# Gated linear attention and a bilinear feed-forward layer on one core: the first two chunks stage by stage over the batch rows, weights issued between their loads, and the y matmuls of a row grouped by tile mode

## The chip, the cores and the metric

The kernel runs on one core of one Trainium2 chip. The metric is the device time of one execution in microseconds (us); the median of several executions is given with the range. A verdict compares the mean time of one kernel's fast runs with the mean of the fast runs of the kernel before in the same rounds; so a ratio is not quite the ratio of the medians that are quoted. A run is called slow when it lies over 1.5% above the fastest of the same kernel, and slow runs take no part in a ratio. The granted clock is the share of full speed at which TensorE was let run; "half clock" below is a granted clock of 0.5.

## The reference, cut to what matters

```python
# q, k, v, alpha: (4, 8, 768, 48) float32, alpha in 0.8 .. 1.0
for t in range(S):
    state = alpha[:, :, t, :, None] * state + einsum('bhd,bhe->bhde', k[:, :, t], v[:, :, t])
    y[:, :, t] = einsum('bhd,bhde->bhe', q[:, :, t], state)
x = y.transpose(0, 2, 1, 3).reshape(3072, 384)
out = ((x @ w_a) * (x @ w_b)) @ w_out      # w_a, w_b: 384 x 1536, w_out: 1536 x 384
```

## The kernel before

The 768 tokens are cut into six chunks of 128. Within a chunk the recurrence becomes matmuls: with beta the running product of alpha (the exponential of a cumulative sum of logarithms), Q' = q·beta and K' = k/beta, y is the masked product of scores with v plus Q' times the state that came in. Heads are padded from 48 to 64 columns so that two fit on 128 partitions; there are four such pairs. A "row" below is one of the four batch rows of a chunk. A "bank" is one of the named tiles ("t1", "t2", "se", "so", four of "f") that TensorE writes results into and that another engine must have read before they are written again. A matmul's tile mode is the part of TensorE's array that it uses: the full width, or 48 of its columns.

```python
def stA(ch, b):                                     # cumulative sum of the logs, two exponentials
    p = ps.tile([C, 512], F32, name="t2")[:, :H * D]
    nc.tensor.matmul(p, lhsT=ut_f32, rhs=ch.la[:, b], start=True, stop=True)
    nc.scalar.activation(out=ch.beta[:, b], in_=p, func=AF.Exp)
    nc.scalar.activation(out=ch.invb[:, b], in_=p, func=AF.Exp, scale=-1.0)
def stB(ch, b):                                     # K' and Q' on GpSimd, v to bf16 on VectorE
    ...
def stC(ch, b):                                     # 8 transposes into bank "t1", one copy (qk)
    ...
def stD(ch, b):                                     # 8 score matmuls into "se" and "so", two masks
    ...
    nc.vector.tensor_mul(ch.me, se, mask4)
    nc.vector.tensor_mul(ch.mo, so, mask4)
def stY(ch, b):
    y = ps.tile([C, P2, C], F32, name="t2")
    for p in range(P2):                             # a full-width matmul and two 48-wide ones, in turn
        nc.tensor.matmul(y[:, p, :], lhsT=Sb[:, b, p, :], rhs=ch.qkD[:, 0, p, :], start=True, stop=False, ...)
        nc.tensor.matmul(y[0:D, p, :], lhsT=ch.vb[:, b, 2 * p, :], rhs=ch.me[:, p, :], start=False, stop=True, ...)
        nc.tensor.matmul(y[DP:DP + D, p, :], lhsT=ch.vb[:, b, 2 * p + 1, :], rhs=ch.mo[:, p, :], ...)
    nc.scalar.activation(out=ch.xT[:, :, b, :], in_=y[:, :KT, :], func=AF.Copy)
    nc.scalar.activation(out=ch.y3[:, b, :], in_=y[:, KT, :], func=AF.Copy)
def fill(ch):                                       # the 4th head pair goes into the padding rows of xT
    for r in range(2):
        for t in range(KT):
            nc.sync.dma_start(out=ch.xT[r * DP + D:(r + 1) * DP, t], in_=ch.y3[...])
...
for b in range(B):                                  # chunk 0, one row after the other
    logs(c0, b); stA(c0, b); stB(c0, b)
    ...
    if b == 1: load_ab(0)                           # a quarter of w_a and w_b, by columns
    if b == 2: load_ab(1)
    stC(c0, b); stD(c0, b); stY(c0, b)
fill(c0)
for b in range(B): stK(c0, b)                       # state update
load_ab(2); load_ab(3)
for i in range(4): load_o(i)
logs(chunks[1]); ...
for c in range(NCH):                                # dense layer of chunk c, attention of c+1 between its blocks
    for f in range(NFF):
        ff_a(ch, f); ...; ff_b(ch, f)
    for m in range(B):
        ff_o(ch, m)
        if n2 is not None and m >= 2: stA(n2, m - 2); stB(n2, m - 2)
```

("..." marks what is left out.) The dense layer of a chunk is twelve blocks (three matmuls with w_a, three with w_b) and four output groups of twelve matmuls with w_out.

Of the kernel before, what the change touches and what calls it, by code (L numbers as in the profile page):

```python
# [15 lines left out]
def kernel(  # L16
# [43 lines left out]
    Qp, Kp = [], []  # L60
    for i in range(2):
        t = cst.tile([C, B, H, DP], BF16, name=f"Qp{i}")
        nc.vector.memset(t, 0.0)
        Qp.append(t)
        t = cst.tile([C, B, H, DP], BF16, name=f"Kp{i}")
        nc.vector.memset(t, 0.0)
        Kp.append(t)

    wa_t = cst.tile([128, KT, d_ff], BF16, name="wa_t")
    wb_t = cst.tile([128, KT, d_ff], BF16, name="wb_t")  # L70
    wo_t = cst.tile([128, NFF, d_model], BF16, name="wo_t")
    WS = d_ff // 4

    def load_ab(i):
        fs = slice(i * WS, (i + 1) * WS)
        for w, t in ((moe_w_a, wa_t), (moe_w_b, wb_t)):
            two = w[:KT * 2 * D, fs].rearrange("(t r d) f -> r d t f", r=2, d=D)
            rest = w[KT * 2 * D:, fs].rearrange("(r t g) f -> r g t f", r=2, g=G)
            for r in range(2):
                nc.gpsimd.dma_start(out=t[r * DP:r * DP + D, :, fs], in_=two[r])  # L80
                nc.gpsimd.dma_start(out=t[r * DP + D:(r + 1) * DP, :, fs], in_=rest[r])

    def load_o(i):
        n = NFF // 4
        nc.gpsimd.dma_start(out=wo_t[:, i * n:(i + 1) * n, :],  # L85
                            in_=moe_w_out[i * n * 128:(i + 1) * n * 128, :].rearrange("(k p) f -> p k f", p=128))


    class Chunk:
# [8 lines left out]
    def alloc_loads(ch):  # L98
        ch.a = ld.tile([C, B, H, D], F32, name="a_t")
        ch.k = ld.tile([C, B, H, D], F32, name="k_t")  # L100
        ch.q = ld.tile([C, B, H, D], F32, name="q_t")
        ch.v = ld.tile([C, B, H, D], F32, name="v_t")

    def load(ch, b):
        if b == 0:
            alloc_loads(ch)
        sl = slice(ch.c * C, (ch.c + 1) * C)
        for t, src in ((ch.a, alpha), (ch.k, k), (ch.q, q), (ch.v, v)):
            nc.sync.dma_start(out=t[:, b], in_=src[b, :, sl, :].rearrange("h s d -> s h d"))

    def logs(ch, b=None):
        if b is None or b == 0:
            ch.la = wk.tile([C, B, H * D], F32, name="la")
            ch.beta = wk.tile([C, B, H * D], F32, name="beta")
            ch.invb = wk.tile([C, B, H * D], F32, name="invb")
            ch.vb = wk.tile([C, B, H, D], BF16, name="vb")
            ch.bl = wk.tile([C, B, P2], F32, name="bl")
            ch.xT = wk.tile([128, KT, B, C], BF16, name="xT")
            ch.y3 = wk.tile([128, B, C], BF16, name="y3")
        if b is None:  # L120
            nc.scalar.activation(out=ch.la.rearrange("p b f -> p (b f)"), in_=ch.a.rearrange("p b h d -> p (b h d)"), func=AF.Ln)
        else:
            nc.scalar.activation(out=ch.la[:, b], in_=ch.a[:, b].rearrange("p h d -> p (h d)"), func=AF.Ln)  # L123

    def stA(ch, b):
        p = ps.tile([C, 512], F32, name="t2")[:, :H * D]
        nc.tensor.matmul(p, lhsT=ut_f32, rhs=ch.la[:, b], start=True, stop=True)  # L127
        nc.scalar.activation(out=ch.beta[:, b], in_=p, func=AF.Exp)  # L128
        nc.scalar.activation(out=ch.invb[:, b], in_=p, func=AF.Exp, scale=-1.0)  # L129

    def stB(ch, b):
        i = ch.c % 2
        nc.gpsimd.tensor_mul(Kp[i][:, b, :, :D], ch.k[:, b], ch.invb[:, b].rearrange("p (h d) -> p h d", h=H))  # L133
        nc.gpsimd.tensor_mul(Qp[i][:, b, :, :D], ch.q[:, b], ch.beta[:, b].rearrange("p (h d) -> p h d", h=H))  # L134
        nc.vector.tensor_copy(ch.vb[:, b], ch.v[:, b])

    def decay(ch):
# [6 lines left out]
            nc.sync.dma_start(out=ch.bl[r * DP:r * DP + D].rearrange("d b a -> d (b a)"),  # L144
                              in_=row[:, :, r, :].rearrange("o a d -> d (o a)"), allow_slow_non_contiguous=True)

    def stC(ch, b):
        i = ch.c % 2
        t = ps.tile([C, 2, P2, C], BF16, name="t1")
        for p in range(P2):  # L150
            for j, src in enumerate((Qp[i], Kp[i])):
                nc.tensor.transpose(t[:, j, p, :], src[:, b, 2 * p:2 * p + 2, :].rearrange("s h d -> s (h d)"), ident)  # L152
        ch.qk = wk.tile([C, 2, P2, C], BF16, name="qk", bufs=3)
        nc.vector.tensor_copy(ch.qk.rearrange("p j a s -> p (j a s)"), t.rearrange("p j a s -> p (j a s)"))  # L154

    def stD(ch, b):
        se = ps.tile([C, P2, C], F32, name="se")
        so = ps.tile([C, P2, C], F32, name="so")
        for p in range(P2):
            nc.tensor.matmul(se[:, p, :], lhsT=ch.qk[0:DP, 1, p, :], rhs=ch.qk[0:DP, 0, p, :], start=True, stop=True)  # L160
            nc.tensor.matmul(so[:, p, :], lhsT=ch.qk[DP:2 * DP, 1, p, :], rhs=ch.qk[DP:2 * DP, 0, p, :], start=True, stop=True)  # L161
        ch.me = wk.tile([C, P2, C], BF16, name="me")
        ch.mo = wk.tile([C, P2, C], BF16, name="mo")
        nc.vector.tensor_mul(ch.me, se, mask4)  # L164
        nc.vector.tensor_mul(ch.mo, so, mask4)  # L165
        ch.qkD = ch.qk

    def stY(ch, b):
        y = ps.tile([C, P2, C], F32, name="t2")
        for p in range(P2):  # L170
            nc.tensor.matmul(y[:, p, :], lhsT=Sb[:, b, p, :], rhs=ch.qkD[:, 0, p, :], start=True, stop=False, skip_group_check=True)  # L171
            nc.tensor.matmul(y[0:D, p, :], lhsT=ch.vb[:, b, 2 * p, :], rhs=ch.me[:, p, :], start=False, stop=True, skip_group_check=True)  # L172
            nc.tensor.matmul(y[DP:DP + D, p, :], lhsT=ch.vb[:, b, 2 * p + 1, :], rhs=ch.mo[:, p, :], start=False, stop=True, skip_group_check=True)  # L173

        nc.scalar.activation(out=ch.xT[:, :, b, :], in_=y[:, :KT, :], func=AF.Copy)  # L175
        nc.scalar.activation(out=ch.y3[:, b, :], in_=y[:, KT, :], func=AF.Copy)

    def fill(ch):
        for r in range(2):
# [36 lines left out]
    def ff_o(ch, m):  # L216
        op = ps.tile([128, NT], F32, name="f", bufs=4)[:, :d_model]
        for f in range(NFF):
            nc.tensor.matmul(op, lhsT=ch.prod[:, f, m * C:(m + 1) * C], rhs=wo_t[:, f, :], start=(f == 0), stop=(f == NFF - 1))  # L219
        ot = wk.tile([128, d_model], F32, name="ot", bufs=3)  # L220
        nc.scalar.activation(out=ot, in_=op, func=AF.Copy)  # L221
        nc.sync.dma_start(out=out[m * S + ch.c * C:m * S + (ch.c + 1) * C, :], in_=ot)


    for b in range(B):
        load(chunks[0], b)
    for b in range(B):
        load(chunks[1], b)
    c0 = chunks[0]
    for b in range(B):  # L230
        logs(c0, b)
        stA(c0, b)
        stB(c0, b)
        if b == B - 1:
            decay(c0)
        if b == 1:
            load_ab(0)
        if b == 2:
            load_ab(1)
        stC(c0, b)  # L240
        stD(c0, b)
        stY(c0, b)
    fill(c0)
    for b in range(B):
        stK(c0, b)
    load_ab(2)
    load_ab(3)
    for i in range(4):
        load_o(i)
    logs(chunks[1])  # L250
    stA(chunks[1], 0)
    stB(chunks[1], 0)
    stA(chunks[1], 1)
    stB(chunks[1], 1)

    for c in range(NCH):
        ch = chunks[c]
        nx = chunks[c + 1] if c + 1 < NCH else None
        n2 = chunks[c + 2] if c + 2 < NCH else None
        todo = {}  # L260
        if nx is not None:
            todo = {
                0: lambda: stA(nx, 2), 1: lambda: stB(nx, 2), 2: lambda: (stC(nx, 0), stA(nx, 3)),
                3: lambda: (stD(nx, 0), stB(nx, 3), decay(nx)), 4: lambda: stC(nx, 1), 5: lambda: (stY(nx, 0), stK(nx, 0), stD(nx, 1)),
                6: lambda: stC(nx, 2), 7: lambda: (stY(nx, 1), stK(nx, 1), stD(nx, 2)), 8: lambda: stC(nx, 3),
                9: lambda: (stY(nx, 2), stK(nx, 2), stD(nx, 3)), 11: lambda: (stY(nx, 3), fill(nx), stK(nx, 3)),
            }
        for f in range(NFF):
            ff_a(ch, f)
            if n2 is not None and f == 0:  # L270
                for b in range(B):
                    load(n2, b)
            if n2 is not None and f == NFF - 1:
                logs(n2)
            if f in todo:
                todo[f]()
            ff_b(ch, f)
        for m in range(B):
            ff_o(ch, m)
            if n2 is not None and m >= 2:  # L280
                stA(n2, m - 2)
                stB(n2, m - 2)


# [28 lines left out]
```

## Time and profile before

| | before |
|---|---|
| median of 3 (range) | 281.64 us (280.61 to 281.82) |
| span of the profiled execution | 280.6 us |
| TensorE busy | 231.5 us, 82% |
| chunk 0's dense layer begins | 60.83 us |
| chunk 1's dense layer begins | 109.56 us |
| period from one dense layer to the next, chunks 1 to 3 | 36.69 us |
| chunk 4's period; chunk 5 to the end | 33.79; 27.19 us |

Read it as two parts. From 109.56 us to the last store, TensorE is busy for 98% or more of each period, and a period has a price in TensorE work. Before that TensorE waits, and the question is for whom.

### The profile page before, as it was taken

What the parts mean: (1) busy time and instruction counts of PE and PEld (TensorE: products, weight loads), DVE (VectorE), ACT (ScalarE), POOL (GpSimd) and SP (SyncE); (2) the same over time, 40 slices, a digit from 0 to 9 for tenths busy, and PEclk for the clock granted to TensorE, in tenths of its full rate; (3) what the DMA queues carried; (4) which work ended last, traced back from release to release, by engine and by line L of the source; (5) the groups of instructions that cost most, each with busy time, mean ns of one, the idle gap of its engine ahead of it and who ended that gap; (6) DMA issues with size and microseconds to landing.
All of it is one profiled execution on the core that took longest, in us unless ns stands there. A gap on an engine that the chain in (4) does not pass through costs nothing.

```text
span 280.6 us, 4180 instructions
## 1 busy us (share of the span) xinstructions
PE 231.5 (82%) x1520; PEld 120.6 (43%) x1520; DVE 120.3 (43%) x213; ACT 122.8 (44%) x219; POOL 89.7 (32%) x134
## 2 busy tenths in 40 slices
PE   2435344584399999999999999999999999999994
PEld 0203122231245554555544555545555455454452
DVE  7303030422057820867505767047861267503420
ACT  5061533552033367533765336563365644424431
POOL 2217352297942114604127023082040730000000
PEclk9999999999579999999999999999999999999999
DMA  8999961079994005982039940289501200021002
GB/s 155 215 211 208 192 87 2 7 145 209 196 184 66 1 12 158 218 176 19 5 123 205 188 62 2 99 184 204 94 2 52 75 2 0 4 71 56 0 32 84
DMA packets 117503, 28.07 MB, mean 100 GB/s; under 512 B 109221, under 2 KB 117477, under 8 KB 117482
## 3 DMA queue, kind: packets, MB, share of 16 engines
q1 hardware_dynamic: 112298, 24.25, 42.2%
q0 software_dynamic: 5184, 3.54, 8.7%
q8 instruction: 12, 0.20, 0.3%
q14 instruction: 9, 0.07, 0.1%
HBM read 25.98 MB, written 4.75 MB: 110 GB/s over the span
## 4 chain that ended last, share of the span: by engine, by line
PE 76%; POOL 6%; issue 6%; ACT 4%; DMA 3%; DVE 3%; POOLq 0%; DVEq 0%; ACTq 0%
PE f L213 17%; PE f L219 17%; PE f L205 15%; PE t L127 7%; PE t L172 6%; PE t L171 5%; PE t L152 5%; PE se L160 3%; PE t L189 2%; DMA wa_t<-in_moe_w_a_dram 2%; POOL Kp L133 2%; ACT invb L129 2%; POOL Qp L134 2%; DMA a_t<-in_alpha_dram 1%; POOL wo_t L85 1%
## 5 line engine op out<-in xcount | busy, mean ns | idle before, releaser
L205 PE MATMUL f<-xT,wa_t 128*128 128x512 bf16 x216 | 59.7, 386 | 0.0
L213 PE MATMUL f<-xT,wb_t 128*128 128x512 bf16 x216 | 59.5, 385 | 0.0
L219 PE MATMUL f<-wo_t,prod 128*128 128x384 bf16 x288 | 48.4, 326 | 0.0
L133 POOL TENSOR_TENSOR Kp<-k_t,invb 128x384 bf16<-128x384 f32 x24 | 23.8, 992 | 65.6 <-ACT invb L129 65.5
L195 POOL TENSOR_TENSOR Sb<-tmp,bl 48x192 bf16<-48x192 f32 x40 | 20.1, 502 | 70.6 <-DMA bl<-row 43.4
L127 PE MATMUL t<-la,ut_f 128*128 128x384 f32 x48 | 26.9, 649 | 15.8 <-ACT la L123 12.2
L219 PEld LDWEIGHTS <-prod 128*128 128x128 bf16 x288 | 28.2, 98 | 20.2 <-issue 0.9
L154 DVE COPY qk<-t 128x1024 bf16<-128x1024 bf16 x24 | 16.5, 687 | 42.4 <-PE t L152 41.8
L205 PEld LDWEIGHTS <-wa_t 128*128 128x128 bf16 x216 | 21.4, 99 | 27.0 <-issue 2.8
L152 PE MATMUL t<-ident,Qp 128*128 128x128 bf16 x96 | 15.2, 237 | 20.3 <-POOL Qp L134 20.3
L175 ACT ACTIVATE xT<-t 128x384 bf16<-128x384 f32 x24 | 11.7, 487 | 40.3 <-PE t L173 40.3
L213 PEld LDWEIGHTS <-wb_t 128*128 128x128 bf16 x216 | 18.8, 99 | 20.7 <-issue 4.1
L172 PE MATMUL t<-me,vb 128*48 128x128 bf16 x96 | 23.6, 246 | 2.3 <-DVE me L164 2.3
L173 PE MATMUL t<-mo,vb 128*48 128x128 bf16 x96 | 23.6, 246 | 1.3 <-DVE mo L165 1.3
L194 DVE TENSOR_TENSOR tmp<-t,Sb 48x192 f32<-48x192 f32 x40 | 14.2, 355 | 24.3 <-PE t L189 20.3
L134 POOL TENSOR_TENSOR Qp<-q_t,beta 128x384 bf16<-128x384 f32 x24 | 24.3, 1012 | 0.0
L221 ACT ACTIVATE ot<-f 128x384 f32<-128x384 f32 x24 | 11.8, 491 | 25.2 <-PE f L219 25.2
L171 PE MATMUL t<-qk,Sb 128*128 128x128 bf16 x96 | 22.8, 237 | 0.0
L152 PEld LDWEIGHTS <-Qp 128*128 128x128 bf16 x96 | 10.1, 107 | 27.6 <-POOL Qp L134 25.4
L128 ACT ACTIVATE beta<-t 128x384 f32<-128x384 f32 x24 | 11.8, 490 | 22.4 <-PE t L127 22.3
L164 DVE TENSOR_TENSOR me<-se,mask 128x512 bf16<-128x512 f32 x24 | 16.6, 692 | 9.4 <-PE so L161 7.5
L127 PEld LDWEIGHTS t<-la,ut_f 128*128 128x128 f32 x48 | 9.1, 232 | 21.8 <-ACT invb L129 8.8
(182 smaller groups left out, 297.3 us busy)
## 6 DMA issues: line engine op xcount, KB each, us to landing
a_t<-in_alpha_dram SPq DMA_DIRECT2D x24, 192.0 KB, 3.9
k_t<-in_k_dram SPq DMA_DIRECT2D x24, 192.0 KB, 3.8
q_t<-in_q_dram SPq DMA_DIRECT2D x24, 192.0 KB, 3.8
v_t<-in_v_dram SPq DMA_DIRECT2D x24, 192.0 KB, 3.9
out_dram<-ot SPq DMA_DIRECT2D x24, 192.0 KB, 1.9
wo_t<-in_moe_w_out_dram POOLq DMA_DIRECT2D x4, 288.0 KB, 8.4
wa_t<-in_moe_w_a_dram POOLq DMA_DIRECT2D x8, 108.0 KB, 4.6
wb_t<-in_moe_w_b_dram POOLq DMA_DIRECT2D x8, 108.0 KB, 5.4
```

What stands on the lines that cost most here:

```text
L127: nc.tensor.matmul(p, lhsT=ut_f32, rhs=ch.la[:, b], start=True, stop=True)
L133: nc.gpsimd.tensor_mul(Kp[i][:, b, :, :D], ch.k[:, b], ch.invb[:, b].rearrange("p (h d) -> p h d", h=H))
L134: nc.gpsimd.tensor_mul(Qp[i][:, b, :, :D], ch.q[:, b], ch.beta[:, b].rearrange("p (h d) -> p h d", h=H))
L152: nc.tensor.transpose(t[:, j, p, :], src[:, b, 2 * p:2 * p + 2, :].rearrange("s h d -> s (h d)"), ident)
L164: nc.vector.tensor_mul(ch.me, se, mask4)
L171: nc.tensor.matmul(y[:, p, :], lhsT=Sb[:, b, p, :], rhs=ch.qkD[:, 0, p, :], start=True, stop=False, skip_group_check=True)
L172: nc.tensor.matmul(y[0:D, p, :], lhsT=ch.vb[:, b, 2 * p, :], rhs=ch.me[:, p, :], start=False, stop=True, skip_group_check=True)
L173: nc.tensor.matmul(y[DP:DP + D, p, :], lhsT=ch.vb[:, b, 2 * p + 1, :], rhs=ch.mo[:, p, :], start=False, stop=True, skip_group_check=True)
L195: nc.gpsimd.tensor_mul(Sb[rs, b, :, r * DP:r * DP + D], tmp[rs], ch.bl[rs, b, :].rearrange("p (a o) -> p a o", o=1).broadcast_to([D, P2, D]))
L205: nc.tensor.matmul(ap, lhsT=wa_t[:, kk, f * 128:(f + 1) * 128], rhs=x[:, kk, :], start=(kk == 0), stop=(kk == KT - 1))
L213: nc.tensor.matmul(bp, lhsT=wb_t[:, kk, f * 128:(f + 1) * 128], rhs=x[:, kk, :], start=(kk == 0), stop=(kk == KT - 1))
L219: nc.tensor.matmul(op, lhsT=ch.prod[:, f, m * C:(m + 1) * C], rhs=wo_t[:, f, :], start=(f == 0), stop=(f == NFF - 1))
```

## The change

Its intent: fill the start-up, in which TensorE is two to five tenths busy, by running each stage of chunks 0 and 1 for all four rows before the next stage; have the weights ready when the dense layer can start; and stop paying for mode switches in y. In chunks 0 and 1 the fill transfers go as well: the fourth head pair's part of v and of the state is copied into columns 48 to 63 of the other heads (the tiles vz and Sz), so that y's matmuls write the padding rows themselves. The diff, cut to its core:

```diff
-    def load_ab(i):                                    # four column slices
+    def load_ab(lo, hi):                               # two: 0..384 and 384..1536
...
     def stY(ch, b):
         for p in range(P2):
-            nc.tensor.matmul(y[:, p, :], lhsT=Sb[...], rhs=..., start=True, stop=False, ...)
-            nc.tensor.matmul(y[0:D, p, :], ...)
-            nc.tensor.matmul(y[DP:DP + D, p, :], ...)
+            nc.tensor.matmul(y[:, p, :], lhsT=Sb[...], rhs=..., start=(p == 0), stop=False, ...)
+        for p in range(P2):
+            nc.tensor.matmul(y[0:D, p, :], ...)
+            nc.tensor.matmul(y[DP:DP + D, p, :], ...)
...
+    def stYz(ch, b, tag):          # chunks 0 and 1: y from spread copies vz, Sz; no y3, no fill
...
+    def first(ch):
+        for b in range(B):
+            mulK(ch, b, nc.gpsimd)
+        yield
+        if ch.c:
+            for b in range(B):
+                mulQ(ch, b, nc.vector if b < 2 else nc.gpsimd)
+            stC(ch, 0, "t1")
+            stC(ch, 1, "t2")
+            yield
+            stD(ch, 0)
+            stC(ch, 2, "f", act=True)
+            stC(ch, 3, "f", act=True)
+            stD(ch, 1, ("t1", "t2"))
+        else:
...
+        stD(ch, 2)
+        stD(ch, 3, ("t1", "t2"))
+        for b in range(B):
+            nc.scalar.activation(out=ch.vb[:, b], in_=ch.v[:, b], func=AF.Copy)
+            nc.vector.tensor_copy(vz[:, b, :, :, D:], ...)
+        for b in range(B):
+            stYz(ch, b, "f")
...
+    load_all(c0)                   # a, then k and q, then v; two rows per transfer
+    logs(c0, 0, 2)
+    logs(c0, 2, 4)
+    for b in range(B):
+        stA(c0, b, "f")
+    g0 = first(c0)
+    next(g0)                       # K' of four rows on GpSimd
+    load_ab(0, 384)
+    load_ab(384, d_ff)
+    for i in range(3):
+        load_o(4 * i, 4 * i + 4)
+    nc.gpsimd.memset(c1.a[0:1, 0, 0, 0:1], 0.0)      # holds chunk 1's loads until here
+    list(g0)
+    load_all(c1)
...
+        if c == 0:
+            for b in range(B):
+                h[2 * b + 2] = [K(c0, b)]
+            h[NFF - 1] = [lambda: logs(nx)]
+            h[NFF] = [... four sums, into banks t2, se, so, t1 ...]
...
+        elif c == 1:
+            h = {0: [K(ch, 0), K(ch, 1), lambda: logs(nx)], 1: [K(ch, 2), K(ch, 3)], 2: [A(nx, 0), Bm(nx, 0)], ...
+                 5: [A(nx, 3), Bm(nx, 3), lambda: decay(nx), Cm(nx, 0)], ...
+        elif nx is not None:
+            h = {0: [A(nx, 3), Bm(nx, 3), lambda: decay(nx)], 1: [Cm(nx, 0)], ...
+            if c > 0:
+                h.setdefault(NFF - 1, []).append(lambda: logs(n2))
+                for b in range(3):                   # a sum after each of three output groups
+                    h.setdefault(NFF + b, []).extend([A(n2, b), Bm(n2, b)])
```

## The prediction

> **What bounds the kernel now.** I read the page first, then its rows of 40 slices, then the chain of waits, then the timeline of the first 112 us engine by engine, and last the busy time per stretch of the dense part.
>
> ```profile
> PE   2435344584399999999999999999999999999994
> POOL 2217352297942114604127023082040730000000
> DMA  8999961079994005982039940289501200021002
> ```
>
> A slice is 7.0 us. TensorE is the bound from slice 12 on; before that, for some 75 us, it is two to five tenths busy although the kernel has 231.5 us of TensorE work in 280.6 us. So there are two parts with different limits: a start-up that TensorE waits through, and a dense part that it fills.
>
> ```profile
> 27.91 1.28 ACT L123 ACT_TABLE_LOAD   x1
> 29.74 1.28 ACT L128 ACT_TABLE_LOAD   x1
> 32.42 0.99 POOL Kp L133
> 34.41 1.05 PE t L152 x8
> 35.48 0.70 DVE qk L154
> 37.48 0.69 DVE mo L165
> 40.56 1.28 ACT L123
> ...
> 63.09 5.80 DMA wa_t<-in_moe_w_a_dram
> 69.18 1.56 POOL wo_t L85 x2
> 74.55 1.03 PE t L152 x8
> ```
>
> (First two lines from the timeline, the rest from the chain of waits.) A batch row of chunk 0 goes Ln table, Ln, Exp table, cumulative sum, two Exps, Kp and Qp on GpSimd, transposes, copy, scores, two masks, y, and only then does the next row's table load begin: 27.91 to 40.56 is 12.65 us for one row, four times in sequence, to 53. Then the state update and, on GpSimd, the second half of the weights are issued; GpSimd's next Kp and Qp stand behind those issues until 74.5, and TensorE stands behind Qp with the dense layer only just begun (8.38 us idle before the transpose at 74.55). Chunk 1's dense layer starts at 109.56 us. That is the number to move.
>
> ```profile
> 105.87:142.56 36.69, 36.04 (x258) 19.26 (x257) 19.60 (x36) 18.97 (x35) 11.85 (x16) 1.00 0.53 111
> 142.56:179.25 36.69, 36.04 (x257) 19.26 (x257) 19.60 (x36) 18.97 (x35) 11.85 (x16) 1.00 0.53 111
> 253.57:276.92 23.35, 23.34 (x120) 11.56 (x118) 8.24 (x12) 9.12 (x16) 0.00 (x0) 1.00 0.10 35
> ```
>
> (Stretch, its length, busy us of PE, PEld, DVE, ACT, POOL, clock, DMA share, GB/s.) A chunk period is 36.69 us and TensorE is 98% busy in it; the last chunk, with no attention left, takes 23.35. So attention costs 13.3 us of TensorE per period, and any such us saved shortens the end.
>
> ```profile
> 83.25 0.22 PE L171 MATMUL t<-qk,Sb 128*128 128x128 bf16 x1
> 83.40 0.24 PE L172 MATMUL t<-me,vb 128*48 128x128 bf16 x1
> 83.41 0.24 PE L173 MATMUL t<-mo,vb 128*48 128x128 bf16 x1
> 83.57 0.23 PE L171 MATMUL t<-qk,Sb 128*128 128x128 bf16 x1
> 84.91 0.22 PE L160 MATMUL se<-qk 64*128 64x128 bf16 x1
> 84.97 0.22 PE L160 MATMUL se<-qk 64*128 64x128 bf16 x1
> ```
>
> Starts, not durations, tell the price. Score matmuls of one shape follow each other every 0.055 us. In y a full-width matmul and the pair of 48-wide ones alternate, and each switch takes 0.15 to 0.17 us: 83.25 to 83.57 for one head pair.
>
> **What the Trainium skill says.** "TensorEngine Tiling (Array Packing)", Key Properties: changing the tiling mode drains TensorE. The trace agrees: about 0.16 us per switch against 0.055. "TensorE: Matmul & The Clock Gate", Part 1: the array runs at half clock until it has been busy for about 3.4 us, and again after such an idle time. The trace agrees: transposes start every 0.106 us at 34.4 and every 0.056 at 81.5; the sparse start-up runs cold. "ScalarE: Activation LUTs", Table sets: batch by set. Each load takes 1283 ns here, and chunk 0 alone has eight of them. "DMA: Bandwidth & Descriptors", Queues, rings and completion order: engines round-robin between queues by packet. The trace agrees roughly: q/k/v/alpha loads alone move about 214 GB/s; weights alone 0.37 MB in 36 to 39 us, some 123 GB/s written; together (26 to 28 us) 0.23 MB weights and 0.21 MB loads per 2 us. So weights lose about a tenth to company, loads lose half.
>
> **The change, part by part.**
>
> *Chunk 0 by stages.* Loads come as alpha, k, q, v in 0.39 MB pieces, at 214 GB/s and 2.1 us latency (from the first load, 0.74 to 3.72): alpha at 4.7 and 6.5, k01 8.4, q01 10.2, k23 12.0, q23 14, v by 18 to 20, since weights join. ACT: two Lns end 7.35, one Exp table to 8.65, eight Exps 0.41 apart, done by 12. GpSimd: Kp 0 to 3, 0.95 each, the last released by k23: 13.95. Then DVE becomes the slow engine; I place its instructions in program order: Qp 0, 1 to 11.2 (0.5 each, worked out from the 0.53 that 512 elements stream in); qk copies to 13.5 behind cold transposes; me/mo of rows 0, 1 (four at 0.61) to 15.9; Qp 2, 3 to 16.9; cold transposes, qk3 to 19.1; scores; me/mo of rows 2, 3 from 19.4 to 21.9; small vz copies to 22.6. The y matmuls of four rows, about 0.8 us each cold, end near 25, xT at 25.7. The six fill transfers (3.76 us of issue plus landing) are gone for these chunks, paid in chunk 0 by 24 small matmuls on spread copies of v (vz). Dense chunk 0 can begin at about 26 instead of 60.8.
>
> *Weights.* Issued from 13.95, 0.565 us each, traffic from 16. The first 384 columns (0.59 MB) land near 21.5. Semaphores of eight transfers are reused, so the second set waits for the first's landings and the first w_out issue for the second's; the second set (1.77 MB at 123 GB/s, 14.4 us) lands near 36. Chunk 0's first three blocks are done by 31 (the clock is cold at first), then TensorE waits until 36 for w_b. The remaining nine blocks at 1.3, K of four rows and about 2 us of cold clock: 50. w_out (1.18 MB) lands near 47, no wait.
>
> *Chunk 1.* Its loads are held until all weights are issued, near 30, at half rate to 47: alpha 40, k and q by 51, v by 54. Ln at 49 to 51.8, sums on TensorE to 54.5 in four banks, Exps to 56.7, GpSimd Kp and two Qp to 59.1, four output matmul groups (1.95 each) around them to 61.3. After that everything is exposed: transposes, then DVE's eight masks 0.61 apart, 61.8 to 66.6, vz to 67.4, y to 69.2, xT to 69.8. Chunk 1's dense layer starts near 70.5, against 109.56: 39 us gained.
>
> *Chunk 1's period.* It now holds all of chunk 2's attention (sums, 2.6, were partly earlier before), K of its own rows (1.1, and two waits of 0.84 as at 53.76), so 23.4 + 2.8 + 2.6 + transposes 1.8 + scores 1.45 + y 2.6 + K 1.1 + three sums 1.95, about 37.7 us; before 36.7. Loss 1.
>
> *Later chunks.* y in one mode per row: 4 x 0.055 + switch 0.10 + 4 pairs x 0.055 + switch 0.10, about 0.65 us instead of 4 x 0.33 = 1.32. Saves 0.67 per row, 2.7 per period. The sums now lie one to an output group, so the waits for their bank (0.34 + 0.32 in every period) go: 0.65. A period becomes about 33.4; chunk 4's, which does not issue sums, about 30.2.
>
> *Sum.* 70.5 + 37.7 + 33.4 + 33.4 + 30.2 + 23.4 + 3.6 (last store, as before) = 232.2 us of span; the timed runs lie 1 us above the span (281.64 against 280.6). About 233.
>
> **The rivals.**
> 1. *DMA is the new bound.* Chunk 0, the weights and chunk 1 need 14.7 + 29 + 14.7 us of nearly full DMA, so nothing can have chunk 1 complete before about 54. For: the DMA row already shows 9s through the start. Against: my masks on DVE end 12 us later than v. If loads or weights run 15% slower, chunk 0's dense layer slips by 2 to 4 us and chunk 1 with it: 236 to 240. If the 1152-column rows go faster than the 384-column ones (larger packets), 229.
> 2. *DVE masks and copies bound both attention stages.* This is in my sum already; if GpSimd and DVE disturb each other, or the copies on ACT queue behind Exps, each stage loses 2 to 3 us: 238.
> 3. *The 48-wide pairs do not follow at 0.055.* No trace here shows two such pairs in a row. At 0.11, y saves 0.45 per row: 236; if their weight loads eat it all, 244.
> 4. *TensorE goes cold in the waits* (31 to 36, and 62 to 67), which makes 2 to 4 us more than I counted.
> 5. *The gain is given back in later periods*, because chunk 2's attention, fitted within one period, delays its own dense layer by its fill transfers. For: only three output groups lie behind the last y. Against: 3 x 1.95 plus two sums is 7.2 us, and copies, issue and landing took about 6.5. Up to 3 us.
>
> **Range and chances.** The start-up gain is large whichever rival holds; even all of them together leave 250. Most errors point upward by 3 to 6 us, a few (faster packets, shorter DVE work) downward by 5. So 224 to 244 for 8 in 10. Faster by over 2% (under 276): 0.97; within 2%: 0.02; slower: 0.01.
>
> **What would show it.** Right: first dense matmul at 24 to 29 us and a wait on w_b's second set around 31 to 36; chunk 1's first dense matmul at 67 to 74 us, released by the xT copy behind DVE's masks; y rows of about 0.65 us in the later chunks; a period of 33 to 34; no wait of a sum for invb. Wrong: TensorE waiting for alpha, k or v of chunk 1; a wait on w_out; y rows still over 1 us; the period still above 35; a hole before chunk 2's dense layer with the fill as its releaser.

## The result, and the profile after

| | before | after |
|---|---|---|
| median (range) | 281.64 us | 239.25 us (238.92 to 240.27, 4 runs) |
| ratio of fast runs | | 0.851 (0.848 to 0.854) |
| span of the profiled execution | 280.6 us | 237.6 us |
| chunk 0's dense layer begins | 60.83 | 26.35 |
| chunk 1's dense layer begins | 109.56 | 71.66 |
| periods of chunks 1, 2, 3 | 36.69 each | 40.20, 34.36, 34.35 |
| chunk 4's period; chunk 5 to the end | 33.79; 27.19 | 29.86; 27.17 |

The 43.0 us of span come out of this table: 37.9 up to chunk 1's dense layer, minus 3.5 in chunk 1's period, plus 2.3 in each of two periods, plus 3.9 in chunk 4's. So the change is mostly a change of the start.

First the page's rows of 40 slices after the change (5.9 us each), tenths of busy time; the third row is the granted TensorE clock.

```profile
PE   0755839989776899989999989999899999999993
POOL 2379431309005681329311336212256000000000
PEclk9976897999979999999999999999999999999999
DMA  8999999996999109993399922599721000130012
```

The row of 2s to 5s that TensorE had for most of the first twelve slices is gone. Two dips remain once the dense layers have begun: the 3 of slice 5 (counted from 0; 30 to 36 us), and the 7, 7 and 6 of slices 10 to 12 (59 to 77 us). The clock row has 6s and 7s in slices 2, 3, 6 and 11, where it had one pair of 5 and 7 before. That is no loss of clock, for the earlier row does not show the start: it has a 9 at 34 us, where transposes start every 0.106 us, and after the change they start every 0.106 us at a clock of 0.5 (from 12.3 us) and every 0.056 at 1.00 (from 17.8). Up to the first change of clock that a trace recorded (63.4 us before, 8.8 after) its 9s say nothing.

The chain of waits after the change, in order of time (start, length, what was waited on):

```profile
6.63 6.73 DMA k_t<-in_k_dram
...
13.50 1.90 POOL Kp L136 x2
15.39 4.88 DMA wa_t<-in_moe_w_a_dram
...
24.50 10.35 DMA wb_t<-in_moe_w_b_dram
...
34.98 0.81 PE f L295 x3
...
62.47 0.68 DVE me L178
...
66.14 0.17 DVE vz L256
...
71.66 0.82 PE f L287 x3
```

Where the chain before went from one row's Ln table to the next row's, it now goes k's load, K' on GpSimd, the weights' issue behind it, the second slice of w_b, the dense layer, and in chunk 1 DVE's masks. Attention of chunk 0 is not on it at all: the dense layer began at 26.35 but stood 3.55 us at 31.4 for w_b.

A row of y, chunk 2's first (TensorE's timeline: start, length, line, operation):

```profile
89.26 0.39 PE L192 MATMUL t<-qk,Sb 128*128 128x128 bf16 x4
89.58 0.24 PE L194 MATMUL t<-me,vb 128*48 128x128 bf16 x1
...
89.92 0.34 PE L271 MATMUL t<-vb,Kp 128*128 128x96 bf16 x4
```

From 89.26 to the next group of matmuls is 0.66 us. Before, one head pair alone took 0.32.

The busy time per stretch, for the periods of chunk 1, chunk 2 and chunk 4 (start:end, length, busy us of PE, PEld, DVE, ACT, POOL, then clock, DMA share, GB/s):

```profile
71.66:111.86 40.20, 36.70 (x278) 20.11 (x279) 24.99 (x48) 25.04 (x43) 21.16 (x30) 1.00 0.82 124
111.86:146.22 34.36, 33.34 (x259) 18.31 (x257) 19.34 (x36) 18.96 (x35) 11.99 (x18) 1.00 0.77 130
180.57:210.43 29.86, 29.86 (x236) 16.59 (x234) 15.71 (x24) 12.51 (x26) 2.74 (x3) 1.00 0.09 29
```

TensorE's work in an ordinary period fell from 36.04 to 33.34 us, which is 2.7 us, four rows of 0.67. But it idles 1.0 us of it, where it idled 0.65 before; in chunk 1's period it idles 3.5. The view of waits names them, first for chunk 1's period and then for chunk 2's (waiter, released by, us in total, times, longest):

```profile
PE t L271 <- DVE tmp L276: 1.7, 2, 0.9
PE t L131 <- ACT beta L133: 1.3, 2, 0.9
PE f L287 <- DVE xT L217: 0.7, 1, 0.7
PE t L131 <- ACT y L198: 0.5, 1, 0.5
```

```profile
PE t L131 <- ACT la L127: 0.7, 1, 0.7
PE t L131 <- ACT beta L133: 0.3, 1, 0.3
```

Line 131 is the cumulative sum, line 271 the state update; the wait for xT ends with the layer's first matmul and so lies ahead of the period, and the other three make its 3.5 us. The first new wait (0.7 for la) is for Ln: the sums now begin right behind the first output group, while Ln was left in block 11, and it has a table load of 1.28 us and 1.48 us of work ahead of it on ScalarE.

### The profile page after: what moved, and what is told of

It is laid out like the page before. It is cut to its first block, busy times and chain, and to the rows that moved or that the text cites. A ratio compares the mean times of both kernels' runs of the same rounds, so it can differ in the third digit from the quotient of the medians.

```text
span 237.6 us, 4081 instructions
## 1 busy us (share of the span) xinstructions
PE 206.5 (87%) x1544; PEld 114.4 (48%) x1544; DVE 123.8 (52%) x225; ACT 117.2 (49%) x211; POOL 75.0 (32%) x112
## 4 chain that ended last, share of the span: by engine, by line
PE 72%; DMA 9%; ACT 6%; POOL 3%; issue 3%; DVE 3%; SPq 2%; ACTq 0%; POOLq 0%
PE f L295 19%; PE f L287 19%; PE f L301 15%; PE t L131 6%; DMA wb_t<-in_moe_w_b_dram 4%; PE t L161 3%; DMA k_t<-in_k_dram 3%; SPq L111 2%; PE se L174 2%; DMA wa_t<-in_moe_w_a_dram 2%; PE t L194 2%; ACT la L127 2%; PE t L271 2%; ACT L127 2%; PE t L192 1%
## 5 line engine op out<-in xcount | busy, mean ns | idle before, releaser
L131 PE MATMUL t<-la,ut_f 128*128 128x384 f32 x36 | 15.4, 509 | 4.7 <-ACT la L127 2.2
L139 POOL TENSOR_TENSOR Qp<-q_t,beta 128x384 bf16<-128x384 f32 x18 | 18.3, 1021 | 0.0
L167 DVE COPY qk<-t 128x1024 bf16<-128x1024 bf16 x18 | 12.3, 687 | 3.7 <-PE t L161 3.7
L179 DVE TENSOR_TENSOR mo<-so,mask 128x512 bf16<-128x512 f32 x20 | 13.6, 680 | 0.0
L161 PEld LDWEIGHTS <-Kp 128*128 128x128 bf16 x96 | 9.8, 102 | 1.9 <-issue 0.2
L139 DVE TENSOR_TENSOR Qp<-q_t,beta 128x384 bf16<-128x384 f32 x6 | 4.7, 822 | 11.3 <-DMA q_t<-in_q_dram 6.7
L132 ACT ACTIVATE invb<-t 128x384 f32<-128x384 f32 x18 | 8.9, 494 | 3.1 <-PE t L131 2.8
L131 PEld LDWEIGHTS t<-la,ut_f 128*128 128x128 f32 x36 | 6.1, 189 | 9.0 <-ACT beta L133 4.0
L144 DVE CAST vb<-v_t 128x384 bf16<-128x384 f32 x16 | 6.6, 460 | 6.6 <-DMA v_t<-in_v_dram 6.6
L161 PE MATMUL t<-ident,Qp 128*128 128x128 bf16 x72 | 9.9, 219 | 0.0
## 6 DMA issues: line engine op xcount, KB each, us to landing
k_t<-in_k_dram SPq DMA_DIRECT2D x3, 768.0 KB, 10.5
```

The source lines that it names most:

```text
L139: eng.tensor_mul(Qp[ch.c % 2][:, b, :, :D], ch.q[:, b], ch.beta[:, b].rearrange("p (h d) -> p h d", h=H))
L161: nc.tensor.transpose(t[:, j, p, :], src[:, b, 2 * p:2 * p + 2, :].rearrange("s h d -> s (h d)"), ident)
L167: nc.vector.tensor_copy(o_, i_)
L179: nc.vector.tensor_mul(ch.mo[b], so, mask4)
```

## The experiments

Twelve kernels ran, all with correct results. The theory (A): the gain is the start-up, made of stage order and early weights, plus 0.66 us for each grouped row of y; the first dense layer is bound by w_b's arrival and the second by DVE's masks. Rivals: (B) grouping carries little, because weight loads or waits eat it; (C) issuing the weights earlier would have done nearly all of it; (D) DVE's masks bind the first dense layer too.

### Grouping, alone and taken back: e1, e2

e1 puts the grouping alone into the kernel before; e2 takes it out of the kernel after.

```diff
 # e1, on the kernel before
-            nc.tensor.matmul(y[:, p, :], lhsT=Sb[:, b, p, :], rhs=ch.qkD[:, 0, p, :], start=True, ...)
+            nc.tensor.matmul(y[:, p, :], lhsT=Sb[:, b, p, :], rhs=ch.qkD[:, 0, p, :], start=(p == 0), ...)
+        for p in range(P2):
             nc.tensor.matmul(y[0:D, p, :], ...)
 # e2, on the kernel after
-            nc.tensor.matmul(y[:, p, :], lhsT=Sb[:, b, p, :], rhs=ch.qk[b][:, 0, p, :], start=(p == 0), ...)
-        for p in range(P2):
+            nc.tensor.matmul(y[:, p, :], lhsT=Sb[:, b, p, :], rhs=ch.qk[b][:, 0, p, :], start=True, ...)
```

> The kernel before, with only the y matmuls of a batch row grouped by tile mode (four full-width ones, then the eight 48-wide ones). Theory (each mode switch costs about 0.1 us beyond the 0.055 us of a same-mode matmul, and TensorE bounds the dense part): 20 rows of chunks 1 to 5 save 0.67 us each, 13.4 us, and the four start-up rows some 0.9 each on their serial chain, 3.6 us; about 265 us in all, a y row of 0.65 us, a period near 34. Rival (a row is bound by its waits for masks and copies, not by switches): no more than 3 us gained, 279.

> The changed kernel, with only the grouping of the y matmuls undone in chunks 2 to 5 (16 rows). Theory: 16 x 0.67 = 10.7 us slower, about 250 us, all of it in the periods of chunks 1 to 4, the start-up unchanged (chunk 1's dense layer still at about 71.7 us). Rival (the period of the changed kernel is bound by ACT at its boundary, so y has slack): under 4 us slower, 243.

Measured: e1 264.99 us (264.7 to 265.62), ratio 0.943 (0.941 to 0.946). e2 249.77 us (246.81 to 250.61, 6 runs, one of them slow), ratio 0.890 (0.887 to 0.892), so it gives back 10.5 us. Chunk 2's period of e2:

```profile
111.40:148.40 37.00, 35.98 (x259) 19.27 (x256) 19.25 (x36) 19.08 (x35) 11.80 (x17) 1.00 0.67 111
```

That is 2.64 us longer than 34.36, with TensorE's work up by the same 2.64 (35.98 against 33.34): four rows of 0.66, at one for one. Rival B falls. Only e2's start was not as expected: in its trace chunk 1's dense layer begins at 68.56 us and not at 71.66, since w_b's wait ended at 33.64 instead of 34.98 and no half-clock spell followed. Its edit touches nothing before chunk 1's dense layer, so this is how far runs differ by themselves. In e1 the total came out as expected but not its distribution: 8.5 of 17.2 us of span lie before chunk 1's dense layer, where y stands in the chain of each row, and the next two periods fell by only 1.5 and 1.8, since waits took the rest. A right total can hide a wrong split; the split has to be read from the periods.

### The weights earlier, in the kernel before: e3

```diff
         if b == 1:
             load_ab(0)
-        if b == 2:
             load_ab(1)
+        if b == 2:
+            load_ab(2)
+            load_ab(3)
+        if b == B - 1:
+            for i in range(4):
+                load_o(i)
...
-    load_ab(2)
-    load_ab(3)
-    for i in range(4):
-        load_o(i)
```

> The kernel before, with only the issue of the weights moved: all of them are issued by GpSimd between the rows of chunk 0, where it idles, instead of half after the state update. Theory A (the row-by-row chain to 53 us is the larger part of the start-up's cost; the issue order costs the 8.4 us hole of TensorE at 66 to 74.5 plus about 1.5 us of cold clock): about 271 us. Theory B (the weights' issue is what the start-up gain is made of): 250 or less. Theory C (DMA bandwidth is what bounds, so moving issues only moves the queue): above 278.

Measured: 271.56 us (271.13 to 271.91), ratio 0.966 (0.964 to 0.968). Chunk 1's dense layer begins at 98.68 instead of 109.56 and the periods stay at 36.69:

```profile
98.68 0.81 PE L205 MATMUL f<-xT,wa_t 128*128 128x512 bf16 x3
```

So of the 37.9 us of the start, where the weights are issued gives 10.9, in the old order of stages; rival C falls. What is left is the stages' order with what goes with it (merged loads, four banks, two Lns in place of four with fewer table loads, no fill); no run separates these from each other.

### The hold of chunk 1's loads: e4

```diff
-    nc.gpsimd.memset(c1.a[0:1, 0, 0, 0:1], 0.0)
     list(g0)
     load_all(c1)
```

> The changed kernel without the one-element memset that holds chunk 1's loads back until all weights are issued; they then start right behind chunk 0's. Theory (chunk 0's dense layer waits for w_b, and loads in company slow the weights): w_b's second set lands 3 to 4 us later, TensorE's wait for it grows from 3.55 to about 7 us, and the total to about 242. Rival (weights lose only a tenth in company, and chunk 1 is bound by its loads): between 237 and 240, chunk 1 starts earlier or at the same time.

Measured: 243.06 us (240.93 to 245.7), ratio 0.862 (0.858 to 0.868) against 0.851. So the hold is worth about 1.2% of the time of the kernel before, some 3 us. The profiled run was a slow one: in it w_b's wait ended at 36.14 instead of 34.98, and the clock was at half from 67.2 to 84.2 us, where the kernel after had 3.4 us of it. Even the 1.2 us of w_b can't be put down to the hold, because traces of kernels with the same loads and weights have that wait end anywhere from 33.64 (e2) to 36.28 (e7). That the hold helps is shown by the fast runs' times; through what, late weights or clock, stays open.

### Which engine holds each dense layer: e5, e6

Each does one of the two masks twice, in chunk 0 (e5) or in chunk 1 (e6): 4 x 0.6 = 2.4 us more for DVE and nothing else.

```diff
         nc.vector.tensor_mul(ch.me[b], se, mask4)
+        if ch.c == 0:            # e6: ch.c == 1
+            nc.vector.tensor_mul(ch.me[b], se, mask4)
```

> The changed kernel with one of the two mask products of each of chunk 0's four rows done twice on DVE (same result), 4 x 0.60 = 2.4 us more on DVE. Theory (chunk 0's dense layer is bound by the arrival of w_b, with TensorE waiting 3.55 us for it at 31 to 35): the first dense matmul moves from 26.35 to about 28.7, the wait for w_b shrinks by as much, and the total stays within 0.5 us of 239.3. Rival (DVE's chain bounds the start-up): 241.7.

> The same doubling in chunk 1 instead. Theory (after the last output group DVE's masks are the exposed chain that sets when chunk 1's dense layer starts): it starts 2.4 us later than 71.66, at about 74, and the total is about 241.7. Rival (chunk 1 is bound by its loads, by ACT's copies or by TensorE): no later, 239.3.

Measured: e5 237.63 us (236.91 to 237.87), ratio 0.845 (0.842 to 0.847); e6 242.59 us (240.74 to 243.78), ratio 0.862 (0.858 to 0.868). In e6 chunk 1's dense layer began 4.4 us later than in the kernel after (76.09 against 71.66), behind y's wait for DVE:

```profile
76.09 0.82 PE L289 MATMUL f<-xT,wa_t 128*128 128x512 bf16 x3 [0.66 <-DVE xT L219]
```

That is more than the 2.4 us expected. 1.3 us were there already when chunk 0's output groups began (49.45 against 48.18), after a half-clock spell twice as long; with the 2.4 of the masks 0.8 are left, and y ran at half clock for nearly all of its time. In e5 chunk 0's began at 28.90 instead of 26.35, and it cost nothing: rival D falls, w_b's arrival sets this layer. But e5 did not stay at 239.3; it was 1.6 us faster, outside what I had expected, though barely clear of noise (its ratio ends at 0.847, that of the kernel after begins at 0.848, and they ran in different rounds). TensorE's timeline shows what differs between the two profiled runs, first of the kernel after and then of e5 (the bracket is the idle time before and its releaser):

```profile
34.98 0.81 PE L295 MATMUL f<-xT,wb_t 128*128 128x512 bf16 x3 [3.55 <-DMA wb_t<-in_moe_w_b_dram]
```

```profile
34.94 0.81 PE L297 MATMUL f<-xT,wb_t 128*128 128x512 bf16 x3 [1.18 <-DMA wb_t<-in_moe_w_b_dram]
```

w_b comes at the same time. What differs is where TensorE's idle time lies: 3.55 us in one piece, or part of it ahead of the layer. And the five microseconds after it, first of the kernel after and then of e5 (same columns as the stretches above; the number before the DMA share is the granted clock):

```profile
35.00:40.00 5.00, 5.00 (x19) 2.15 (x20) 2.09 (x4) 1.07 (x2) 1.01 (x2) 0.66 1.27 187
```

```profile
35.00:40.00 5.00, 5.00 (x30) 2.43 (x31) 3.30 (x7) 1.79 (x3) 1.14 (x3) 1.00 1.26 189
```

Nineteen matmuls against thirty: after the long wait the clock was granted at half from 36.1 to 39.6 us. Two more runs have a wait of nearly the same length:

```profile
35.38 1.01 PE L297 MATMUL f<-xT,wb_t 128*128 128x512 bf16 x2 [3.35 <-DMA wb_t<-in_moe_w_b_dram]
```

```profile
34.69 0.81 PE L298 MATMUL f<-xT,wb_t 128*128 128x512 bf16 x3 [3.29 <-DMA wb_t<-in_moe_w_b_dram]
```

The first is e6, with a clock of 0.50 in the five microseconds after 35; the second is e10 below, with 1.00. It is tempting to read an edge between 3.29 and 3.35 us out of this, but the traces do not bear it out: there are half-clock spells behind much shorter waits (below). What fits is another measure. In every trace's record of the clock, spells begin and end on a grid of 3.41 us, and what matters is for how much of such a stretch TensorE worked. The stretch before the spell at 36 us and the spell itself, then the stretch before a second spell at 67 us, all in the kernel after; last, e10's stretch at the first place:

```profile
32.73:36.14 3.41, 1.16 (x6) 0.59 (x7) 0.24 (x1) 0.00 (x0) 0.00 (x0) 1.00 1.37 185
36.14:39.55 3.41, 3.41 (x13) 1.40 (x12) 1.85 (x4) 0.62 (x2) 1.01 (x2) 0.50 1.27 184
63.44:66.86 3.42, 1.45 (x27) 1.05 (x28) 3.34 (x9) 1.83 (x5) 0.00 (x0) 1.00 1.46 186
```

```profile
32.75:36.17 3.42, 1.48 (x11) 0.80 (x12) 0.57 (x1) 0.00 (x0) 0.00 (x0) 1.00 1.28 189
```

Busy shares of 0.34 and 0.42 were followed by half clock; 0.43 in e10 and 0.65 in e5 (31.88 to 35.29 us) were not. Over all fourteen traces, from the first recorded change of clock on, a full-clock stretch of this grid with TensorE busy for up to 0.42 of it was followed by half clock every time (24 stretches), one with 0.60 or more never; between 0.43 and 0.57 both occur (0.49 in e5 before half clock, 0.49 in b2 before full). The kernel after has stretches near this border, and where the grid falls is different in each run, which may be why its variants spread as they do.

### Keeping the array busy: e8

New hypothesis: the half-clock spells are worth some 3 us, and filling TensorE's idle time is enough to avoid them. e8 adds matmuls whose result nobody reads: fourteen of 512 columns before the w_b wait and eight before chunk 1's y.

```diff
+    def warm(n, tag):
+        d = ps.tile([C, NT], F32, name=tag, bufs=4 if tag == "f" else 1)
+        for _ in range(n):
+            nc.tensor.matmul(d, lhsT=ident, rhs=c0.xT[:, 0].rearrange("p b s -> p (b s)"), start=True, stop=True)
...
+        if ch.c:
+            warm(8, "f")
         for b in range(B):
             stYz(ch, b, "f")
...
+            h[3] = [lambda: warm(14, "se")]
```

> The changed kernel with dummy matmuls, whose result nobody reads, in TensorE's two waits of the start-up: 14 of 512 columns (3.0 us) while it waits for w_b in chunk 0, 8 (1.7 us) while it waits for vz in chunk 1. Theory (after each wait TensorE runs at half clock for a while: three-matmul groups start 1.28 us apart instead of 0.65 at 36.7 to 39.3, and y rows 1.53 us apart at 66.8 to 69.9): 1.7 us less after the first wait, about 2 after the second, 235.5 in all. Rival (the waits for DVE and DMA behind it take the place of the cold time): under 1 us gained, or the dummies only stand in the way.

Measured: 236.18 us (235.96 to 237.5), ratio 0.842 (0.838 to 0.845). In the trace there is no half-clock spell after 24.9 us; chunk 0's output groups begin 1.95 us earlier (46.23) and chunk 1's dense layer 3.4 earlier:

```profile
68.28 0.82 PE L294 MATMUL f<-xT,wa_t 128*128 128x512 bf16 x3 [0.66 <-DVE xT L217]
```

So useless work made the kernel 3 us faster. The hypothesis stands.

### The order within DVE in chunk 1: e10

In the kernel after, y's first row waits for the small vz copies, which DVE does behind all eight masks. e10 puts them ahead of the masks.

```diff
             stC(ch, 1, "t2")
             yield
+            for b in range(B):
+                nc.vector.tensor_copy(vz[:, b, :, :, D:], ...)
             stD(ch, 0)
...
-            nc.vector.tensor_copy(vz[:, b, :, :, D:], ...)
+            if not ch.c:
+                nc.vector.tensor_copy(vz[:, b, :, :, D:], ...)
```

> The changed kernel with chunk 1's four vz copies moved on DVE ahead of the masks, into its idle time after the qk copies; nothing else. Theory (DVE's order, not its amount of work, is what holds the y matmuls: row 0 waits for vz, which stands behind all eight masks): row 0 of y starts near 64.1 instead of 66.35, the rows follow their masks, chunk 1's dense layer starts near 68 instead of 71.66, and the total is 3 to 4 us less, about 235.7. Rival 1 (only the 0.72 us of the copies themselves leaves the chain): 238.6. Rival 2 (v lands too late and DVE waits for it ahead of the masks): 239.3 or more.

Measured: 236.18 us (234.16 to 237.19), ratio 0.837 (0.833 to 0.842). TensorE's timeline where y begins and where chunk 1's dense layer begins, first of the kernel after, then of e10:

```profile
66.35 0.24 PE L212 MATMUL f<-me,vz 128*64 128x128 bf16 x1 [1.73 <-DVE vz L256]
...
71.66 0.39 PE L287 MATMUL f<-xT,wa_t 128*128 128x512 bf16 x1 [0.66 <-DVE xT L217]
```

```profile
62.58 0.24 PE L212 MATMUL f<-me,vz 128*64 128x128 bf16 x1
...
66.45 0.82 PE L290 MATMUL f<-xT,wa_t 128*128 128x512 bf16 x2 [0.66 <-DVE xT L217]
```

In e10 y's first row has no wait: it needs only its own row's masks, and the other rows' masks run under it. Of the 5.2 us between the two traces, 2.0 are not the edit: e10's masks began at 59.15 instead of 61.13, and this run had no half-clock spell at 36. The remaining 3.2 us fit the 3.1 between the medians. They are two things: counted from the masks, y began 1.8 us sooner, and from there to the dense layer it took 3.87 us instead of 5.31, since it ran at full clock. So 0.72 us of copies in a wrong place held four rows for 1.8 us, and left TensorE idle enough for the half-clock spell that cost the other 1.4.

That spell is the second one named above, and it needed no long wait. The kernel after just before y and during y (stretches):

```profile
61.90:66.35 4.45, 1.86 (x34) 1.10 (x31) 4.41 (x9) 3.37 (x6) 0.00 (x0) 1.00 1.44 187
66.80:71.60 4.80, 4.21 (x58) 3.16 (x54) 1.11 (x2) 0.98 (x2) 0.00 (x0) 0.64 1.20 180
```

The longest wait in the first stretch is 1.73 us, but TensorE is busy in only 1.86 of 4.45, and y then ran at a clock of 0.64: four rows in 4.7 us, against 0.90 us a row in e10.

### Ln earlier: e7

```diff
-            h[NFF - 1] = [lambda: logs(nx)]
+            h[NFF - 2] = [lambda: logs(nx)]
...
-                h.setdefault(NFF - 1, []).append(lambda: logs(n2))
+                h.setdefault(NFF - 2 if c == 1 else NFF - 3, []).append(lambda: logs(n2))
```

> The changed kernel with the Ln of the chunk after next put one or two dense blocks earlier on ACT (block 10 in chunks 0 and 1, block 9 later). Theory (the sums of the next chunk now follow the first output group, and wait for a Ln that ACT ends too late: 0.67 us, then 0.35 us behind the Exps, in each period, 0.88 us in chunk 0): 2 to 4 us faster, 235.5 to 237, periods of about 33.4 instead of 34.36. Rival (the table load then delays the copies of the dense layer and TensorE waits for those instead): no change, 239.

Measured: 237.09 us (236.16 to 239.93), ratio 0.842 (0.839 to 0.845). The profiled run counts as slow (it was 1.6% above the fastest), but its later periods ran at full clock, as the 1.00 in the line shows:

```profile
147.70:181.16 33.46, 33.11 (x257) 18.41 (x256) 19.31 (x36) 18.77 (x35) 11.79 (x17) 1.00 0.75 122
```

33.46 us instead of 34.36: the period that I had predicted is there once the sums no longer wait for Ln. Chunk 1's period did not change (40.2): its idle time has other releasers.

### Loads by row: e9, and a theory that fell

The loads of chunk 0 ran at 0.37 MB per 2 us after the change and 0.43 before; I suspected the merged two-row transfers.

```diff
                 for w in what:
-                    load(ch, w, lo, lo + 2)
+                    for b in (lo, lo + 1):
+                        load(ch, w, b, b + 1)
```

> The changed kernel with the loads of chunks 0 to 2 issued one batch row at a time again (192 KB each, same order and bytes), as the kernel before did. The traces show 0.37 MB per 2 us for the two-row loads of the changed kernel and 0.43 MB for the one-row loads of the kernel before. Theory (the size of the issue is the reason): chunk 0's loads move 0.43 MB per 2 us again, its second pair of Kp starts near 12.2 instead of 13.50, the weights with it, TensorE gets w_b near 33.5 instead of 34.98, and the total is 1 to 2 us less, about 237.7. Rival (the rate differs for another reason, or the weights are not released by it): 239.3.

Measured: 245.58 us median, but three of its four runs were slow; the one fast run took 238.04, so there is no ratio. The trace answers the question of the mechanism all the same: the loads' rate stayed at 0.37 to 0.38 MB per 2 us, and w_b came at 36.33 us, later than 34.98, although K' (12.35) and with it the weights' issue began 1.1 us sooner. The size of an issue is not what slows these loads. The order of the tensors and rows in time is one of the differences that are left; no run tests it.

### Together: b1, b2

b1 joins what had helped: the vz copies first, ten matmuls before the w_b wait, Ln earlier; and two new edits for chunk 1's period, three banks in turn for the sums and the state updates spread over four blocks.

```diff
-        A = lambda x, b: (lambda: stA(x, b))
+        A = lambda x, b: (lambda: stA(x, b, ("se", "so", "t2", "se")[b]))
...
-            h = {0: [K(ch, 0), K(ch, 1), lambda: logs(nx)], 1: [K(ch, 2), K(ch, 3)], 2: [A(nx, 0), Bm(nx, 0)], 3: [A(nx, 1), Bm(nx, 1)],
+            h = {0: [K(ch, 0), lambda: logs(nx)], 1: [K(ch, 1)], 2: [K(ch, 2), A(nx, 0), Bm(nx, 0)], 3: [K(ch, 3), A(nx, 1), Bm(nx, 1)],
```

b2 is b1 with e9's loads by row.

> Everything found together on the changed kernel: vz ahead of the masks in chunk 1; Ln one or two blocks earlier; 10 dummy matmuls in the wait for w_b; the K groups of chunk 1 one to a dense block instead of two (their waits of 0.84 and 0.91 us on DVE go); sums in three banks in turn instead of one (waits of 0.93, 0.5 and 0.35 us on ACT go). If the parts add: chunk 1's dense layer near 66, its period 37 instead of 40.2, the next two 33.1 instead of 34.36, about 228 in all. Rival (a wait removed uncovers the next, ACT's or the fill's): 231 to 234.

> The same with the loads of chunks 0 to 2 by one row. If that part is worth what the single run of it shows, another 1 to 2 us, about 226.5; else as the run without it.

Measured: b1 229.42 us (228.55 to 230.69), ratio 0.815 (0.811 to 0.818); b2 230.39 us (230.14 to 231.74), ratio 0.819 (0.815 to 0.822). b1 beats both kernels; it is 4% faster than the kernel after. b2 is no faster than b1: of its two expected outcomes the 226.5 failed and "as the run without it" came, which agrees with what e9's trace said, now without slow runs. Chunk 1's and chunk 2's periods of b1:

```profile
65.79:104.08 38.29, 35.96 (x275) 20.09 (x280) 26.43 (x48) 24.64 (x43) 20.98 (x29) 1.00 1.02 159
104.08:136.92 32.84, 32.63 (x253) 18.46 (x256) 19.69 (x37) 18.77 (x35) 12.23 (x18) 1.00 0.81 130
```

Chunk 2's period is work to 99% (32.63 of 32.84). In chunk 1's the waits for tmp, for the Exps and for y's copy are gone from the view of waits, and two new ones have come, 1.7 us for DVE's copy of the transposes and 0.4 for Ln; so the period is 38.29 and not the 37 expected, as the rival there had said. That the waits of the sums were for one bank, which an earlier sum's Exps and y's copy held, agrees with the fall from 40.2 to 38.29; which of the two new edits gave how much was not separated.

## Why the prediction was right or wrong

The time is 239.25 against a predicted 233 and a range of 224 to 244: the range holds it, the number is 6.3 us low. By the prediction's own sum of spans:

| term | predicted | measured | off |
|---|---|---|---|
| up to chunk 1's dense layer | 70.5 | 71.66 | +1.2 |
| chunk 1's period | 37.7 | 40.20 | +2.5 |
| two later periods | 2 x 33.4 | 2 x 34.36 | +1.9 |
| chunk 4's period | 30.2 | 29.87 | -0.3 |
| chunk 5 and the last store | 27.0 | 27.2 | +0.2 |
| timed run over span | 1.0 | 1.7 | +0.7 |

The mechanism was right; three terms of the sum were mis-sized. Two small ones are slips of reading: the stretch 253.57:276.92 begins 0.16 us behind the last chunk's first matmul (253.41), and the median was set against the span of a run that itself took 282.33.

- *Chunk 0 by stages, the weights.* Right. The dense layer began at 26.35 (predicted "about 26"), waited for w_b until 34.98 ("until 36"), and its blocks ended at 48.2 ("50"). Two errors cancelled: the weights' issue began at 15.39 instead of 13.95, since k's second half landed at 13.4 and not at 12.0, and the second slices with 1152 columns moved 0.37 MB in 2 us, 186 GB/s, where I had used the 123 of 384 columns, a rate that GpSimd's issuing alone held down (two issues of 0.565 us for 144 KB are at most 130 GB/s). That they cancelled is luck. The second was the downward case of rival 1. e5 shows that w_b, not attention, sets this layer; e3 shows that early weights alone are 10.9 of the 37.9 us.
- *Chunk 1's start.* Right in kind (masks one after the other on DVE, then vz, then y, then the xT copy) and 1.2 us late; the small error is again a balance, since y could begin at 66.35 where I had 67.4 and then took longer. e6 confirms the bound. I had put y's four rows after all the masks without asking whether they have to be there; e10 shows that they don't, which with the clock is worth 3 us. y itself took 4.7 us from 66.35, at reduced clock, where I had 1.8; even at full clock e10's rows are 0.90 us apart, so the matmuls on the spread copies, which only these chunks have, were under-counted.
- *Chunk 1's period.* This is the step with the largest error: "about 37.7 us". It was made of 36.0 of work and 1.7 of waits for tmp; measured were 36.70 and 3.5. The waits for tmp came as predicted (0.84 and 0.91 in the timeline). Left out were those of a sum for the Exps of the sum before it (1.3 in two waits) and for y's copy (0.5), together the 1.8 that the waits are off: I counted work and not banks. The other 0.7 is not more matmuls, since b1 runs the same ones in this period with 35.96 busy; what makes it is not resolved.
- *Later periods.* The grouping term is right (0.66 us a row, 0.67 predicted; e2 gives 2.64 per period). Wrong was "so the waits for their bank (0.34 + 0.32 in every period) go: 0.65". They were replaced: moving the sums ahead put them in front of Ln's end (0.67), and one wait for the bank remained (0.35). e7 removes the first by moving Ln, and the period is then 33.46.
- *The rivals.* Rival 1 was right that DMA binds the first dense layer, but TensorE never waited for chunk 1's loads. Rival 2 holds in chunk 1 and falls in chunk 0. Rival 3 fell: the 48-wide pairs follow each other every 0.06 to 0.07 us. Rival 4 was right in part: e8 gets 3.1 us back, of which the sum had counted about 2. Rival 5 fell: no wait for a fill stands before chunk 2's dense layer.

## What to carry to other kernels

When TensorE waits through a start-up because one row's chain of engines runs after another's, do each stage for all rows, with a bank for each, and place the one transfer that the first dense layer needs by the engine that issues it; then look for what now comes last, because a 0.7 us copy at the end of an engine's list can hold four rows. After moving work to an earlier slot, move its producers too: a wait that was taken away came back as another one, for the Ln that had been early enough before. Sum TensorE's work and its banks: work says what a period can be, bank holders say what it is.

## What the Trainium skill lacked or had wrong

- "TensorEngine Tiling (Array Packing)", Key Properties, says that a mode switch drains TensorE but not what it costs. Here a switch between full-width and 48-wide matmuls took 0.15 to 0.17 us against 0.055 within one mode; six switches fewer in each row of y are 0.66 us, which e2 shows one for one (2.64 us per period of four rows).
- "TensorE: Matmul & The Clock Gate", Part 1, has the half clock return after an idle window of about 3.4 us, and its rule table names gaps over about 3 us. The spells here do lie on a grid of 3.41 us, but no such window had to be idle: TensorE had worked for 0.34 and 0.42 of the two before the spells of the kernel after, the second with no wait over 1.73 us. Part 1 does say that frequent short idles can cost the clock too, but gives no share; the traces here put it between 0.42 (always half clock next) and 0.60 (never).
- "ScalarE: Activation LUTs", Table sets, says that Ln then Exp needs one load, since one set has both. In this build each change between Ln and Exp has a load. And What ACT_TABLE_LOAD costs gives about 2.66 us per switch with a drain of about 1.38; the trace shows Ln ending at 7.90, the load from 7.92 to 9.20, and Exp starting at 9.22: 1.3 us in all.
- "DMA: Bandwidth & Descriptors", Bandwidth, has no rate for transfers that cast. Weights from float32 to bf16 alone moved 124 GB/s as the trace counts them with rows of 384 columns (556 packets for 0.37 MB in 3 us) and 186 GB/s with rows of 1152 (186 packets for the same in 2 us). That the row length makes the difference is not shown: the first rate is close to the 130 GB/s at which GpSimd issued those slices.
